# Moving weight loads to a second DMA queue in fp32, with a replanned instruction order, in a pooled-attention and expert-attention kernel

## The chip, the cores and the metric

The kernel runs on one core of one Trainium2 chip. The metric is the device time of one execution in microseconds (us). Executions are sorted into a fast and a slower state, and only fast ones are compared: the ratios leave slow ones out, while the medians quoted are of all runs. Apart from the whole-run time there is the span in the profile, which is about 1.7 us shorter than the time of the same run.

Engine names: TensorE (PE) multiplies matrices, VectorE (DVE) and ScalarE (ACT) evict and compute element by element, GpSimd (POOL) masks and issues loads, SyncE (SP) issues stores. PEld is TensorE's weight load. PEclk is the clock that TensorE was granted, as a share of full speed.

## The reference, cut to what matters

```python
# B=8 batches, H=8 heads, S=576 positions, D=64; fp32 in and out
k_p = k.reshape(B, H, 72, 8, D).mean(axis=3)        # pool k and v by 8
v_p = v.reshape(B, H, 72, 8, D).mean(axis=3)
x = softmax(q @ k_p^T / 8) @ v_p                    # first attention
x = x.transpose(0, 2, 1, 3).reshape(B, S, 512)
logits = x @ w_gate                                 # 4 experts, the best 2 are used
for e in range(4):                                  # causal attention per expert, width 64
    a = softmax(causal((x @ wq[e]) @ (x @ wk[e])^T / 8))
    out += gate[e] * (a @ (x @ wv[e]) @ wo[e])
```

Each batch brings 3.5 MB of fp32 q, k and v. All weights together are 2.1 MB. They are loaded once and first needed after the first attention of batch 0: before that point the kernel needs k, q and v only.

## The kernel before: the parts that matter

The kernel is scheduled by hand. A string of tokens gives the order; each engine executes its own tokens in that order. `L_q3:0` loads chunk 3 of q of batch 0, `W2:0` loads a weight (0 wq, 1 wk, 2 wv, 3 gate, 4 wo), `c` sorts a loaded weight into the layout that TensorE wants, `PK`, `KT`, `Q`, `E`, `D`, `PV`, `O` are the first attention on TensorE (pool k, transpose, transpose q, scores, denominators, pool v, outputs), `V` and `P` the projections of the experts, and small letters the evictions. A `d` at the end puts an eviction on VectorE.

```python
def load(b, nm, c):                       # one chunk of q, k or v
    ...
    nc.gpsimd.dma_start(out=dst, in_=src)   # fp32 in HBM -> bf16 in SBUF: a casting load

def load_weights(i):
    ...
    nc.gpsimd.dma_start(out=dst, in_=src)   # the same queue, also casting

def order_weights(i):                     # bf16 -> bf16 copies, all on VectorE
    ...

SEQ = """
    H:0 M:0 L_k2:0 L_k0:0 I:0 L_k1:0 L_q3:0 L_q2:0 L_q0:0 L_q4:0 L_q5:0 PK:0@0 L_q1:0 kc:0d
    W2:0 KT:0@0 L_v2:0 kt:0d L_v1:0 W3:0 Q3:0@0 Q0:0@1 L_v0:0 r3:0d Q2:0@2 r0:0 Q1:0@3 r2:0d
    ... o11:0 D2:0@3 x0:0 d2:0 o00:0 W1:0 x2:0 o01:0 W0:0 ...   # wk and wq
    ... W4:0 ...                                                # wo, much later
```

`H` is a block of warm-up matmuls that has TensorE at full clock when the first k arrives. So all loads share one queue, in the order in which they are needed: k, q, then wv, v, and the other weights behind.

The softmax here doesn't subtract the row's maximum and nothing guards it: scores larger than these inputs give would overflow.

## Time and profile before

The median of three runs is 180.87 us (180.75 to 182.9). The profiled execution has a span of 178.7 us.

| stage | what happens | length |
|---|---|---|
| 0 to 30 us | the head: loads, first attention of batch 0, clock mostly at half | 30 us |
| 30 to 173 us | TensorE busy 140.7 of 143 us at clock 1.00 | 143 us |
| 173 to 178.7 us | last evictions and stores | 5.5 us |

These are the lines of the profile's page of the kernel before. The second line is busy time (share of the span) and instruction count of each engine; the next two cut the span into 40 slices, in tenths of busy time and of full clock; then the chain of work that ended last, by engine; then the DMA queues with packets, MB written and share of the 16 engines' span.

```profile
span 178.7 us, 5425 instructions
PE 163.2 (91%) x2143; PEld 96.7 (54%) x2143; DVE 123.5 (69%) x408; ACT 140.0 (78%) x251; POOL 106.6 (60%) x183
...
PE   7729689999999999999999999999999999999870
...
PEclk9955556999999999999999999999999999999997
...
PE 71%; DVE 9%; ACT 7%; POOL 4%; issue 3%; DMA 2%; DVEq 0%; POOLq 0%; ACTq 0%
...
q0 software_dynamic: 78928, 15.21, 102.2%
q1 hardware_dynamic: 5248, 9.44, 14.7%
```

TensorE is the bound except in the first six or seven slices; in most of these its clock is halved. Queue q0 carries the casting loads; its MB are those written, and it reads twice as much. Queue q1 here carries the stores alone.

The stretches of the head, kernel before. Columns: stretch, length, busy time (instructions) of PE, PEld, DVE, ACT, POOL, then granted clock, DMA share, GB/s written.

```profile
10.00:15.00 5.00, 2.50 (x27) 2.14 (x28) 1.02 (x4) 0.64 (x1) 5.00 (x7) 0.50 1.91 150
15.00:20.00 5.00, 3.67 (x31) 1.76 (x31) 0.30 (x1) 4.68 (x7) 4.26 (x6) 0.50 1.84 168
20.00:25.00 5.00, 4.10 (x40) 1.24 (x34) 3.44 (x10) 3.04 (x7) 4.66 (x6) 0.50 2.23 162
25.00:30.00 5.00, 4.98 (x47) 3.79 (x47) 2.38 (x7) 0.97 (x4) 3.98 (x6) 0.50 1.84 179
```

The clock is 0.50 all through. Only in the last of these stretches is TensorE itself the limit (4.98 of 5 us busy).

The timeline of TensorE in the head, kernel before. Columns: start, length, engine, line, operation, operands, count, and in brackets the idle time before and what ended it.

```profile
8.71 0.61 PE L204 MATMUL psum<-kraw_71,poolk 96*32 96x512 bf16 x5 [0.99 <-DMA kraw_71<-in_k_dram]
...
13.26 2.02 PE L208 MATMUL psum<-ident,qraw_68 96*128 96x96 bf16 x23 [1.93 <-DMA qraw_68<-in_q_dram]
...
25.36 2.78 PE L204 MATMUL psum<-wvg,xT_97 128*128 128x260 bf16 x12
...
29.12 1.60 PE L208 MATMUL psum<-ident,qraw_69 96*128 96x96 bf16 x24
```

These four are the landmarks: k is there at 8.7 us, the last q at 13.26 us, the first expert projection starts at 25.36 us, and batch 1 follows at 29.12 us.

### The profile page before, as it was taken

The page shows a single profiled execution, that of the slowest core. Times are in us where ns is not written, and L with a number is a line of the kernel's source. Part 1 is how long each engine was busy: PE and PEld are TensorE (multiplying, and loading weights), DVE is VectorE, ACT ScalarE, POOL GpSimd, SP SyncE. Part 2 cuts the span into 40 slices and gives each one's busy share as a digit, 9 for nine tenths or more (in the row PEclk, how much of TensorE's full clock was granted, in tenths as well). Part 3 has the DMA queues.
Part 4 walks back from the last instruction along what each step waited for, and adds up shares of the span by engine and source line. Part 5 has one row for each costly group of instructions (what it writes and reads, how often), then busy time and mean ns, then how long its engine had stood idle before and what let it go on. Part 6 is the DMA issues. An engine that isn't in the chain of part 4 may idle for free.

```text
span 178.7 us, 5425 instructions
## 1 busy us (share of the span) xinstructions
PE 163.2 (91%) x2143; PEld 96.7 (54%) x2143; DVE 123.5 (69%) x408; ACT 140.0 (78%) x251; POOL 106.6 (60%) x183
## 2 busy tenths in 40 slices
PE   7729689999999999999999999999999999999870
PEld 2516147446575565745666566556655555567530
DVE  5022374686789885994898579968998569498860
ACT  2007914899989878989989889988998999997660
POOL 6999797786699788948999538017131202254000
PEclk9955556999999999999999999999999999999997
DMA  3999999999969999999999998950439010200486
GB/s 32 126 140 163 172 165 178 160 158 144 112 70 148 163 236 206 194 173 273 129 135 167 222 189 89 155 207 5 43 117 226 31 59 6 88 0 6 164 306 238
DMA packets 84202, 25.00 MB, mean 140 GB/s; under 512 B 79312, under 2 KB 79568, under 8 KB 84176
## 3 DMA queue, kind: packets, MB, share of 16 engines
q0 software_dynamic: 78928, 15.21, 102.2%
q1 hardware_dynamic: 5248, 9.44, 14.7%
q8 instruction: 16, 0.26, 0.6%
q14 instruction: 10, 0.08, 0.2%
HBM read 30.42 MB, written 9.44 MB: 223 GB/s over the span
## 4 chain that ended last, share of the span: by engine, by line
PE 71%; DVE 9%; ACT 7%; POOL 4%; issue 3%; DMA 2%; DVEq 0%; POOLq 0%; ACTq 0%
PE psum L204 63%; PE psum L208 8%; DMA qraw_68<-in_q_dram 2%; POOL qraw_68 L112 2%; DVE osc_111 L465 2%; ACT eta_91 L270 2%; ACT etb_101 L420 1%; DVE osc_110 L465 1%; POOL kraw_71 L112 1%; ACT lnz_93 L291 1%; DVE xT_97 L313 1%; ACT ofin L201 1%; ACT rza_95 L294 1%; DVE gt_109 L461 1%; DVE gt_108 L461 1%
## 5 line engine op out<-in xcount | busy, mean ns | idle before, releaser
L437 POOL TENSOR_SCALAR_AFFINE_SELECT etb_100<-etb_100 128x256 bf16<-128x256 bf16 x32 | 12.6, 410 | 28.1 <-ACT etb_100 L420 28.0
L420 ACT ACTIVATE etb_101<-psum 128x1024 bf16<-128x1024 f32 x24 | 23.8, 1029 | 4.2 <-PE psum L204 3.5
L420 ACT ACTIVATE etb_100<-psum 128x1024 bf16<-128x1024 f32 x24 | 23.8, 1027 | 1.2 <-PE psum L204 1.1
L437 POOL TENSOR_SCALAR_AFFINE_SELECT etb_101<-etb_101 128x256 bf16<-128x256 bf16 x32 | 12.7, 411 | 19.8 <-ACT etb_101 L420 15.2
L270 ACT ACTIVATE eta_92<-psum 96x1024 bf16<-96x1024 f32 x16 | 15.7, 1021 | 1.0 <-PE psum L204 0.8
L270 ACT ACTIVATE eta_91<-psum 96x1024 bf16<-96x1024 f32 x16 | 15.6, 1019 | 0.3 <-PE psum L204 0.3
L201 DVE CAST qk_103<-psum 128x512 bf16<-128x512 f32 (+1 forms) x16 | 10.3, 653 | 7.9 <-PE psum L204 7.7
L201 ACT COPY ofin<-psum 128x512 f32<-128x512 f32 (+1 forms) x24 | 13.3, 583 | 2.8 <-PE psum L204 2.6
L112 POOL DMA_DIRECT2D qraw_69<-in_q_dram x18 | 13.9, 774 | 1.0 <-DMA vraw_74<-in_v_dram 1.0
L112 POOL DMA_DIRECT2D qraw_68<-in_q_dram x18 | 13.8, 771 | 0.4 <-issue 0.2
L201 DVE COPY ofin<-psum 128x512 f32<-128x512 f32 (+1 forms) x16 | 10.9, 684 | 1.7 <-PE psum L204 1.6
L201 ACT COPY qT_83<-psum 128x576 bf16<-128x576 bf16 x2 | 1.3, 638 | 12.3 <-PE psum L208 12.3
L204 PEld LDWEIGHTS <-etb_101 128*128 128x128 bf16 x240 | 9.0, 97 | 2.9 <-issue 0.9
L204 PE MATMUL psum<-wvg,xT_97 128*128 128x260 bf16 x60 | 10.3, 314 | 0.0
L112 POOL DMA_DIRECT2D qraw_70<-in_q_dram x12 | 9.2, 774 | 1.3 <-DMA wst_q<-in_moe_wq_dram 1.0
L204 PE MATMUL psum<-vaug_105,etb_101 128*128 128x65 bf16 x240 | 9.8, 193 | 0.0
L204 PEld LDWEIGHTS <-etb_100 128*128 128x128 bf16 x240 | 8.5, 97 | 1.9 <-issue 1.0
L204 PE MATMUL psum<-vaug_104,etb_100 128*128 128x65 bf16 x240 | 9.3, 193 | 0.0
L201 DVE CAST qk_102<-psum 128x512 bf16<-128x512 f32 (+1 forms) x10 | 6.3, 636 | 4.0 <-PE psum L204 4.0
L204 PE MATMUL psum<-wvg,xT_98 128*128 128x260 bf16 x60 | 8.5, 275 | 0.3 <-DVE osc_110 L465 0.3
L204 PE MATMUL psum<-qk_103 64*128 64x64 bf16 (+4 forms) x96 | 8.7, 277 | 0.1
L204 PE MATMUL psum<-qk_102 64*128 64x64 bf16 (+4 forms) x96 | 8.4, 276 | 0.0
(247 smaller groups left out, 472.0 us busy)
## 6 DMA issues: line engine op xcount, KB each, us to landing
out_dram<-ofin SPq DMA_DIRECT2D x32, 256.0 KB, 3.2
kraw_71<-in_k_dram POOLq DMA_DIRECT2D x9, 192.0 KB, 4.4
qraw_68<-in_q_dram POOLq DMA_DIRECT2D x18, 96.0 KB, 4.5
vraw_74<-in_v_dram POOLq DMA_DIRECT2D x9, 192.0 KB, 6.4
kraw_72<-in_k_dram POOLq DMA_DIRECT2D x9, 192.0 KB, 6.6
qraw_69<-in_q_dram POOLq DMA_DIRECT2D x18, 96.0 KB, 6.2
vraw_75<-in_v_dram POOLq DMA_DIRECT2D x9, 192.0 KB, 6.7
qraw_70<-in_q_dram POOLq DMA_DIRECT2D x12, 96.0 KB, 7.4
```

The costliest lines, as they stand in the source:

```text
L112: nc.gpsimd.dma_start(out=dst, in_=src)
L201: (nc.vector.tensor_copy if dve else nc.scalar.copy)(out=out, in_=in_)
L204: nc.tensor.matmul(out=out, lhsT=lhsT, rhs=rhs, start=start, stop=stop)
L208: nc.tensor.transpose(out=out, in_=in_, identity=ident[0:n, 0:n])
L270: nc.scalar.activation(out=eta[:, hp, :, 0:MAIN], in_=psum[0:KR, bank : bank + 2, :], func=EXP, scale=ATT_EXP_SCALE,)
L291: nc.scalar.activation(out=part(lnzs[b % 2], g), in_=z, func=LN)
L294: nc.scalar.activation(out=part(rzas[b % 2], g), in_=part(lnzs[b % 2], g), func=EXP, scale=-1.0)
L313: nc.vector.tensor_tensor(out=xT[:, 2 * g + t, 0:MAIN], in0=psum[:, bank, :], in1=rz[:, g, 0:MAIN], op=MULT)
L420: nc.scalar.activation(out=et[:, ep, :, eo : eo + n], in_=psum[:, bank : bank + 2, 0:n], func=EXP, scale=MOE_EXP_SCALE,)
L437: nc.gpsimd.affine_select(out=blk, in_=blk, pattern=[[0, 2], [1, 128]], compare_op=ISGE, fill=0.0, base=0, channel_multiplier=-1,)
L461: nc.vector.tensor_mul(out=gt[:, :, :, 0], in0=rz[:, :, :, 0], in1=at[b, "G"][:, q0:q1, 2 * ep : 2 * ep + 2].rearrange("p c e -> p e c"),)
L465: nc.vector.tensor_tensor(out=oscs[ep][:, q0:q1, :].rearrange("p c (e d) -> p e c d", e=2), in0=o[:, :, :, 0:HD], in1=gt.to_broadcast([128 ...
```

## The change

The intent: take the weights off the GpSimd queue, where they cost issue time and their place in the order; load them in fp32 by SyncE, which is free until the first store, from the beginning; load k, q and v strictly in turn; keep TensorE busy with filler matmuls in the first waits, so that its clock stays up; use ScalarE less in the head; and plan the whole order again, stores included.

```diff
-    wst = {nm: const.tile([128, E, 2, 2, HD], BF16, name=f"wst_{nm}") for nm in ("q", "k", "v")}
+    wst = {nm: const.tile([128, E, 2, 2, HD], FP32, name=f"wst_{nm}") for nm in ("q", "k", "v")}
+    wst_o = const.tile([128, NEP, DM], FP32, name="wst_o")
...
-        nc.gpsimd.dma_start(out=dst, in_=src)          # in load_weights
+        nc.sync.dma_start(out=dst, in_=src)
+    def open_weights(i):                                # token G: lets SyncE start
+        for t in ([wst["q"], wst["k"]], [wst["v"], wst_g, wst_o])[i]:
+            nc.vector.memset(first(t), 0.0)
-    def order_weights(i):                               # bf16 -> bf16 on VectorE
+    def order_weights(i, dve):                          # fp32 -> bf16, on either engine
...
+    def warm_up(n, bank):                               # token H: n filler matmuls
+        for _ in range(n):
+            nc.tensor.matmul(out=psum[:, bank, :], lhsT=warm[:, 0:128], rhs=warm[:], start=True, stop=True)
...
-        H:0 M:0 L_k2:0 L_k0:0 I:0 L_k1:0 L_q3:0 L_q2:0 L_q0:0 L_q4:0 L_q5:0 PK:0@0 L_q1:0 kc:0d
-        W2:0 KT:0@0 L_v2:0 kt:0d L_v1:0 W3:0 Q3:0@0 Q0:0@1 L_v0:0 r3:0d ...
+        I:0 M:0 L_k0:0 L_k1:0 G0:0 W0:0 L_k2:0 G1:0 W1:0 J:0 W2:0 W3:0 K:0 L_q0:0 c1:0 W4:0
+        L_q1:0 L_q2:0 L_q3:0 L_q4:0 L_q5:0 H20:0@7 PK:0@0 kc:0 L_v0:0 H4:0@7 KT:0@0 L_v1:0
+        L_v2:0 L_k0:1 c0:0 H7:0@7 Q3:0@1 kt:0d L_k1:1 r3:0d c2:0 Q2:0@0 r2:0d Q0:0@2 L_k2:1
+        c3:0d Q1:0@3 r0:0d E3:0@4 e3:0 E2:0@0 L_q0:1 r1:0d H4:0@7 E4:0@4 e2:0 E1:0@2 H1:0@7 ...
```

Cut: the whole remaining order is new too; the softmax logarithm is kept in place of its result (one buffer less); the constants need three affine selects instead of six; one eviction of three instructions became three tokens.

## The prediction

> **What bounds the kernel now.** The span is 178.7 us. TensorE is 91% busy and the chain of waits puts 71% of the span on it. By stretches: from 30 us to its last matmul at 173.2 us TensorE is busy 140.9 of 143 us at granted clock 1.00, so this part is TensorE-bound, with about 2 us of waits, 1.1 of them at 160-170 us. The rest is the head (0-30 us) and the tail (5.5 us from the last matmul to the end). The head is a chain, not TensorE-bound: k lands at 8.7 us, the last q at 13.26, ScalarE exponentials from 15.9, first projection at 25.4 us. The stretches show the granted clock at 0.50 from about 9.5 to 30 us: TensorE waited (12-13 us: no busy time) and then worked at half speed. Of the roughly 15 us of busy time that isn't warm-up before 30 us, most would take half.
>
> **What the change removes.** (a) Five weight issues of 0.7-0.9 us on GpSimd, and four affine selects of 0.2-0.3 us each; three stay, now behind the third k load, so k is issued about 1.6 us earlier. (b) The half clock. From 25.4 to 30.3 us the trace has TensorE saturated at 0.50; at 1.00 that saves about 2.5 us. Earlier half-clock work is mostly hidden by ScalarE. (c) Two or more of batch 0's four qT copies (0.64 us each) leave ScalarE before the first exponential: about 1.3 us. (d) Over the whole kernel some 7 us of evictions move from ScalarE (140 busy) to VectorE (123.5), mostly output copies (24 to 17 on ScalarE).
>
> **What it adds.** Weight reordering now reads fp32: three copies of about 0.6 us on ScalarE, in the wait for q, and about 3.5 us on VectorE. About 21 more filler matmuls of 0.22 us sit in waits. The main cost is contention: 2.1 MB of fp32 weights start at about 3-4 us, beside k and q. The Trainium skill, "DMA: Bandwidth & Descriptors", section "Issuing engines are not separate DMA queues", says a second queue only saves issue time. The trace has the casting loads at 140-180 GB/s written from 8 us on (twice that read), so weights are an estimated 6.5 us of transfer time, shared with q. Estimate: q lands near 15-16.5 us instead of 13.3; v near 20, as before.
>
> **On the critical path.** Later q (+2 to +3) roughly cancels the ScalarE relief and earlier k (-2). The first projection starts within 1.5 us of 25.4. What remains: about 2.5 us from the clock, 0.5-1 from smaller mid-kernel waits, 0.5-1 from a less crowded tail (13 stores among the final tokens now, about 11 then, the last one issued at 175.0 although its tile was ready at 173.8). Sum about 4-5 us.
>
> **Prediction: 176.3 us, 80% range 172.0 to 179.5. Chances: faster by over 2% 0.62, within 2% 0.33, slower 0.05.**
>
> **What would show it.** Windows: granted clock 1.00 from about 8 us on, TensorE busy after 30 us still some 141 us in sum. DMA issues: weights land on the SyncE queue by 14-17 us, q's time to landing rises from 4.5 us to above 6. Timeline: first projection at 24-27 us. Chain: ScalarE exponentials in the head, TensorE afterwards.
>
> **What would make it wrong.** The fillers don't hold the clock: "TensorE: Matmul & The Clock Gate", section "What's actually happening", has it halve after an idle window of about 3.4 us, and the trace halved it after a sparser stretch; a 3-4 us wait for q would do so again, and the gain shrinks to 1-2 us. Or weights barely delay q; then the first projection comes at 23 us and the time is 173. Or the new order has new waits around 50-60 us, where VectorE is 96% busy.

## More of the kernel before

The DMA view of the kernel before, cut to 5 to 20 us: the queue, then the q loads of batch 0 with the median time from issue to landing at the end.

```profile
q0 software_dynamic: 11406, 2.18, 176.0%
...
qraw_68<-in_q_dram POOLq DMA_DIRECT2D x6, 96.0 KB, 4.1
```

## The result, and the profile after

After: median 182.94 us (182.67 to 183.38, four runs). Before, in the same rounds: 180.81 us (179.8 to 182.9, four runs). The ratio is 1.0139, with a 95% interval of 1.0091 to 1.0188. Of the kernel before, the run of 182.9 us is 1.7% above the fastest, which counts as slow, and 1.0139 is the ratio of the means without it (with it, it would be 1.0105). A ratio here is the mean time of one kernel's fast runs over the mean of the other's fast runs of the same rounds, so it is not quite the ratio of the medians that are quoted. The kernel became 1.4% slower, which is within 2% but on the wrong side, and the time lies above the predicted range.

The page of the kernel after, the same lines:

```profile
span 181.2 us, 5407 instructions
PE 162.1 (89%) x2100; PEld 93.9 (52%) x2121; DVE 127.4 (70%) x414; ACT 135.4 (75%) x244; POOL 102.2 (56%) x175
...
PE   7655399999999999999999999999999999999970
...
PEclk9978558999999999999999999999999999999996
...
PE 71%; DMA 13%; DVE 6%; POOL 4%; issue 2%; ACT 1%; POOLq 0%; DVEq 0%; ACTq 0%
...
q0 software_dynamic: 75264, 14.16, 94.6%
q1 hardware_dynamic: 8912, 11.55, 19.6%
```

In the chain that ended last, DMA went from 2% to 13% of the span and ScalarE from 7% to 1%. ScalarE lost 4.6 us of work and VectorE gained 3.9, as intended. The weights are now on q1 (11.55 MB less 9.44 MB of stores is 2.11 MB).

The stretches of the head, kernel after:

```profile
10.00:15.00 5.00, 4.05 (x17) 1.45 (x17) 0.36 (x1) 1.62 (x3) 1.58 (x3) 0.66 1.82 192
15.00:20.00 5.00, 1.06 (x8) 0.44 (x5) 0.00 (x0) 0.62 (x1) 1.54 (x2) 0.79 1.56 240
20.00:25.00 5.00, 3.53 (x26) 2.16 (x28) 2.92 (x7) 1.06 (x2) 3.96 (x5) 0.50 1.84 179
25.00:30.00 5.00, 5.00 (x34) 1.46 (x36) 0.69 (x1) 3.69 (x5) 3.94 (x6) 0.68 2.05 139
```

From 15 to 20 us TensorE is busy for 1.06 of 5 us, VectorE not at all and ScalarE for 0.62: everyone waits for data. The fillers raised the clock in parts, but it is back at 0.50 from 20 to 25 us.

The timeline of TensorE in the head, kernel after:

```profile
10.44 0.59 PE L193 MATMUL psum<-kraw_71,poolk 96*32 96x512 bf16 x4 [2.90 <-DMA kraw_71<-in_k_dram]
...
17.38 0.22 PE L197 MATMUL psum<-ident,qraw_68 96*128 96x96 bf16 x1 [1.59 <-DMA qraw_68<-in_q_dram]
19.95 0.26 PE L197 MATMUL psum<-ident,qraw_68 96*128 96x96 bf16 x1 [2.35 <-DMA qraw_68<-in_q_dram]
...
21.61 1.70 PE L197 MATMUL psum<-ident,qraw_68 96*128 96x96 bf16 x19 [0.36 <-DMA qraw_68<-in_q_dram]
...
32.47 0.28 PE L193 MATMUL psum<-xT_95,wqp_119 128*128 128x64 bf16 x4 [0.20 <-DVE xT_95 L296]
```

The last q is there at 21.6 us instead of 13.26, and the first projection starts at 32.5 us instead of 25.4. The last k came later too (10.4 for 8.7 us), although the last k load was issued earlier.

The DMA view of the kernel after, 5 to 20 us:

```profile
q0 software_dynamic: 6772, 1.13, 96.9%
q1 hardware_dynamic: 3663, 2.11, 59.3%
...
qraw_68<-in_q_dram POOLq DMA_DIRECT2D x6, 96.0 KB, 12.0
```

This is the reading that matters most. Before, the core read 2 × 2.18 = 4.36 MB in this stretch (the casting loads write half of what they read). After, it read 2 × 1.13 = 2.26 MB of loads and 2.11 MB of weights, together 4.37 MB. From 8 to 20 us alone, past a lull in the loads of the kernel before at 6 us, it is 3.64 against 3.54 MB. The second queue added no bandwidth for reading: it gave almost half of it to weights that nobody needed before 25 us. A load of a q chunk took 12.0 us to land instead of 4.1.

The lateness of 7 us at the first projection became only 2.5 us of span. From 30 us on, TensorE had 140.9 us of work before and 142.2 after (some matmul records can be missing from a trace), so by 30 us the new order was behind by little in TensorE work, though it was behind by much in its chain. Which part of the new order does this was not separated.

### The profile page after: what moved, and what is told of

It is laid out like the page before. It is cut to its first block, busy times and chain, and to the rows that moved or that the text cites. A ratio compares the mean times of both kernels' runs of the same rounds, so it can differ in the third digit from the quotient of the medians.

```text
span 181.2 us, 5407 instructions
## 1 busy us (share of the span) xinstructions
PE 162.1 (89%) x2100; PEld 93.9 (52%) x2121; DVE 127.4 (70%) x414; ACT 135.4 (75%) x244; POOL 102.2 (56%) x175
## 3 DMA queue, kind: packets, MB, share of 16 engines
q1 hardware_dynamic: 8912, 11.55, 19.6%
HBM read 30.42 MB, written 9.44 MB: 220 GB/s over the span
## 4 chain that ended last, share of the span: by engine, by line
PE 71%; DMA 13%; DVE 6%; POOL 4%; issue 2%; ACT 1%; POOLq 0%; DVEq 0%; ACTq 0%
PE psum L193 62%; PE psum L197 8%; DMA qraw_68<-in_q_dram 7%; DMA qraw_69<-in_q_dram 3%; DMA qraw_70<-in_q_dram 3%; POOL qraw_68 L112 2%; PE psum L187 2%; POOL kraw_71 L112 1%; DVE xT_95 L303 1%; DVE ofin L190 1%; DVE vaug_103 L190 1%; DVE osc_109 L458 0%; ACT rza_93 L284 0%; DVE W L349 0%; DVE qk_101 L190 0%
## 5 line engine op out<-in xcount | busy, mean ns | idle before, releaser
L427 POOL TENSOR_SCALAR_AFFINE_SELECT etb_98<-etb_98 128x256 bf16<-128x256 bf16 x32 | 12.5, 409 | 26.1 <-ACT etb_98 L410 25.7
L427 POOL TENSOR_SCALAR_AFFINE_SELECT etb_99<-etb_99 128x256 bf16<-128x256 bf16 x32 | 12.5, 410 | 19.4 <-ACT etb_99 L410 18.6
L190 DVE COPY ofin<-psum 128x512 f32<-128x512 f32 (+1 forms) x23 | 15.1, 682 | 2.2 <-PE psum L193 2.2
L187 PE MATMUL psum<-warm 128*128 128x512 bf16 x40 | 13.4, 485 | 1.6 <-DVE poolk L151 1.3
L197 PE MATMUL psum<-ident,qraw_68 96*128 96x96 bf16 x72 | 5.8, 227 | 5.1 <-DMA qraw_68<-in_q_dram 5.1
L112 POOL DMA_DIRECT2D kraw_72<-in_k_dram x9 | 6.9, 769 | 4.3 <-DMA qraw_68<-in_q_dram 4.3
L193 PE MATMUL psum<-qk_101 64*128 64x64 bf16 (+4 forms) x96 | 9.2, 277 | 0.0
L187 PEld LDWEIGHTS <-warm 128*128 128x128 bf16 x41 | 4.4, 117 | 9.2 <-issue 6.0
L193 PE MATMUL psum<-vaug_103,etb_99 128*128 128x65 bf16 x240 | 8.6, 193 | 0.1
L193 PE MATMUL psum<-wvg,xT_96 128*128 128x260 bf16 x60 | 8.7, 274 | 0.0
L193 PEld LDWEIGHTS <-etb_99 128*128 128x128 bf16 x240 | 8.0, 97 | 1.2 <-issue 1.2
L112 POOL DMA_DIRECT2D vraw_74<-in_v_dram x9 | 6.9, 771 | 2.9 <-DMA qraw_68<-in_q_dram 2.1
```

Source lines behind the costliest of these rows:

```text
L187: nc.tensor.matmul(out=psum[:, bank, :], lhsT=warm[:, 0:128], rhs=warm[:], start=True, stop=True)
L190: (nc.vector.tensor_copy if dve else nc.scalar.copy)(out=out, in_=in_)
L193: nc.tensor.matmul(out=out, lhsT=lhsT, rhs=rhs, start=start, stop=stop)
L197: nc.tensor.transpose(out=out, in_=in_, identity=ident[0:n, 0:n])
L427: nc.gpsimd.affine_select(out=blk, in_=blk, pattern=[[0, 2], [1, 128]], compare_op=ISGE, fill=0.0, base=0, channel_multiplier=-1,)
```

## The experiments

**Theory 1 (contention):** the weights in fp32 on the second queue take the bandwidth that k and q need, and this alone turns a gain into a loss. **Rival A (copies):** the weight copies, now on ScalarE and waiting for slow weights (10.03 us at the first one, and the eviction of pooled k stands behind it), hold the head. **Rival B (plan):** the new order or the fillers are worse by themselves. **Rival C (format):** it is fp32 instead of casting, not the queue.

### 1. The new plan with the weights back on the loads' queue (a_wcast)

```diff
-        nc.sync.dma_start(out=dst, in_=src)     # staging FP32
+        nc.gpsimd.dma_start(out=dst, in_=src)   # staging BF16
- ... G0:0 W0:0 L_k2:0 G1:0 W1:0 J:0 W2:0 W3:0 K:0 L_q0:0 c1:0 W4:0 ...
+ ... L_q5:0 W2:0 H20:0@7 ... L_v1:0 W3:0 L_v2:0 W0:0 W1:0 L_k0:1 ...
+ ... o20:0 c0:0 c1:0d c2:0 c3:0d PK:1@0 ... L_v2:1 W4:0 ...
```

> The changed kernel, but the weights go back to bf16 casting loads on the GpSimd queue in the places they had before (wv after q, gate between the v loads, wq and wk after v, wo later); their reorder copies come later to fit. Theory 1 (the early fp32 weights take half of the transfers while q streams in): the last q lands at 13-14 us instead of 21.6, first projection at 23-25 us instead of 32.5, and since the rest of the changed kernel needs 143 us to its last matmul, the time is 174-177 us. Theory 2 (the replanned order itself is worse, the weights don't matter): first projection still after 28 us, time 181-184 us.

Measured: 177.76 us against 179.58 before in the same rounds, ratio 0.9882 (0.9822 to 0.9942). The timeline of TensorE in this kernel:

```profile
12.49 0.98 PE L197 MATMUL psum<-ident,qraw 96*128 96x96 bf16 x19 [0.46 <-DMA qraw<-in_q_dram]
26.24 0.61 PE L193 MATMUL psum<-xT,wqp 128*128 128x64 bf16 x8
```

The last q is there at 12.5 us and the first projection starts at 26.2. Both the projection (expected at 23 to 25 us) and the time (174 to 177) miss theory 1's figures a little, but are far from those of the rival. With the weights back in their place in one queue, the plan of the kernel after is faster than the kernel before. That speaks for theory 1 and against rival B.

### 2. Only the second queue, in the old plan (b_wsp)

```diff
- ... L_k0:0 I:0 L_k1:0 ...
+ ... L_k0:0 I:0 G:0 W0:0 W1:0 W2:0 W3:0 W4:0 L_k1:0 ...   # fp32, by SyncE
- W2:0 / W3:0 / W1:0 / W0:0 / W4:0 at their old places
+ c3:0                                  # one more copy on VectorE, for wo
```

(The logarithm is kept in place, as in the change, to make room for the fp32 staging.)

> The kernel before, with nothing changed but the weights: fp32 on the SyncE queue, released at about 3.4 us. Theory 1: q lands after 19 us instead of 13.3, first projection 5-8 us later, time 185-188 us. Theory 2: within 1 us of 180.8.

Measured: 188.29 us against 179.58, ratio 1.0458 (1.0396 to 1.0519); the median is just above the expected 185 to 188. TensorE's two landmarks, its waits (total, times, longest), and the queues from 5 to 20 us in this kernel:

```profile
20.45 2.02 PE L215 MATMUL psum<-ident,qraw 96*128 96x96 bf16 x23 [1.86 <-DMA qraw<-in_q_dram]
32.20 2.78 PE L211 MATMUL psum<-wvg,xT 128*128 128x260 bf16 x12
...
PE psum L215 <- DMA qraw<-in_q_dram: 5.2, 2, 3.3
PE psum L211 <- DMA kraw<-in_k_dram: 5.0, 1, 5.0
...
q0 software_dynamic: 7102, 1.19, 102.1%
q1 hardware_dynamic: 3664, 2.11, 55.6%
```

The last q comes at 20.45 us and the first projection starts at 32.20, so the head is moved as in the kernel after, with the old order and none of its new copies on ScalarE. Queue q0 wrote 1.19 MB from 5 to 20 us and q1 2.11 MB, nearly the division of the kernel after. The early loads on the second queue alone are enough for the damage. In the old plan they cost 4.6%. In the new plan they cost about 2.6% (1.0139 against the 0.9882 of a_wcast, from different rounds): the plan itself gains the 1.2% of a_wcast, and only the rest of the difference is delay that the new order hides.

### 3. Only the copies later (a_clate)

```diff
- ... L_q0:0 c1:0 W4:0 ... L_k0:1 c0:0 H7:0@7 ... r3:0d c2:0 Q2:0@0 ... L_k2:1 c3:0d Q1:0@3 ...
+ ... o20:0 c0:0 c1:0d c2:0 c3:0d PK:1@0 ...
```

> The changed kernel with its early fp32 weights, only the reorder copies moved behind the first batch's exponentials, so that ScalarE no longer waits for wq before it evicts the pooled k. Theory 1: kp is evicted at about 11 us instead of 12.6, but q still lands at 21-22 us and the time stays within 1 us of 182.9. Theory 2 (ScalarE waiting for weights is the cause): 2-4 us faster.

Measured: 183.38 us, ratio 1.0216 (1.0169 to 1.0263) against the kernel before. TensorE's waits for q add up to 7.9 us. ScalarE no longer waits for weights in front of pooled k, and nothing is won. Rival A falls.

### 4. The second queue, but started later (a_wlate, a_wlate2)

```diff
- ... G0:0 W0:0 L_k2:0 G1:0 W1:0 J:0 W2:0 W3:0 K:0 L_q0:0 c1:0 W4:0 ...
+ ... r0:0d G1:0 G0:0 W2:0 W3:0 W0:0 W1:0 W4:0 E3:0@4 ...    # SyncE starts once q is transposed
+ ... o20:0 c0:0 c1:0d c2:0 c3:0d PK:1@0 ...                # a_wlate2: c4:0d moved here too
```

> The changed kernel, fp32 weights still on the SyncE queue, but released only when q of the first batch has been transposed and copied; reorder copies later. Theory 1: q lands at 13-14 us; the weights now share with v and the second batch, so PV is 1-3 us later than in the run with casting weights; time 175-179 us. Rival (it is the SyncE queue or the fp32 copies that cost, not when the weights are sent): no gain over the changed kernel, 181-184 us.

> The late release on the SyncE queue again, without the flaw of the first try, where the copy of wv stood ahead of the eviction of the pooled v on VectorE and held it 6 us: now all reorder copies come after the outputs of the first attention. Theory 1: the pooled v is evicted at about 17 us, but weights that share with the second batch's loads land late (wk near 29 us, as in the first try), so the first projection is at 28-31 us and the time 179-182 us. If the second queue were harmless once q is in, first projection at 23-25 us and 175-177 us.

Measured: a_wlate 183.01 us, ratio 1.0204 (1.0153 to 1.0255). Theory 1 had expected 175 to 179, so this was a miss, and the rival's figure, 181 to 184, was met. Partly it was a fault of the edit: the copy of wv stood ahead of the eviction of pooled v on VectorE, and wv landed late, so TensorE waited 6.2 us for pooled v. The second edit took that away and still has 183.05 us, ratio 1.0205 (1.0112 to 1.0298), a little above its expected 179 to 182. So a late start does not make the second queue harmless. The waits of TensorE in a_wlate2, and its queues from 14 to 30 us:

```profile
PE psum L193 <- ACT wqp L190: 5.4, 1, 5.4
PE psum L193 <- ACT wkp L190: 2.5, 1, 2.5
...
q0 software_dynamic: 7460, 1.34, 102.5%
q1 hardware_dynamic: 3509, 1.82, 54.9%
```

In a_wcast, in the same stretch, all of it through one queue:

```profile
q0 software_dynamic: 13385, 2.71, 195.2%
```

Here q is in time (12.5 us), and now the weights are late: the copies of wq and wk release the first projections. From 14 to 30 us this kernel read 2 × 1.34 MB of loads and 1.82 MB of weights, 4.50 MB together; a_wcast read 2 × 2.71 = 5.42 MB in the same stretch through one queue. The two queues moved not even as much as one. So theory 1 needs a sharper form. The point is not that weights must keep away from q. All loads up to the first projection share one bandwidth, and a second queue beside a full first one shares it with loads of the next batch that are not yet due, whichever of the two is wanted first. In one queue the order of the tokens decides, and a_wcast has an order that fits the deadlines. (This reading is argued from the two kernels; no run changed the sharing alone.)

### 5. fp32 or the queue (a_wpool32)

As a_wcast, with the staging in fp32 and the copies casting: plain loads of 512 KB, in the GpSimd queue.

```diff
-        nc.sync.dma_start(out=dst, in_=src)     # staging FP32, order as in a_wcast
+        nc.gpsimd.dma_start(out=dst, in_=src)
```

> As the run with casting weights (177.8 us), in the same places of the GpSimd queue, but the weights stay fp32 and are cast by the reorder copies. If what counts is where the weights stand in the order of transfers and not the cast: q lands at 12-13 us, time 177-178.5 us. If the fp32 format itself costs (twice the bytes written, slower copies): 179-183 us.

Measured: 179.18 us, ratio 0.9979 (0.9898 to 1.006). The last q is there at 12.36 us and the first projection starts at 26.39, as in a_wcast. So fp32 does not make the loss (rival C falls as its cause); the second queue does, with the place in the order of transfers that it gives the weights. Whether fp32 costs about 1% against casting stays open: the time lies in the range expected for a format that costs (179 to 183), but the intervals of the two ratios overlap, and they ran on different chips.

### 6. The fillers and the clock (a_nofill, b_fill)

```diff
- H4:0@7 H7:0@7 H4:0@7 H1:0@7 H4:0@3 H1:0@3       # a_nofill: after, without these 21 fillers
+ F5 before PK, F4 before KT, F9 before Q3, F4 before D1, F2 before PV, F2 before O01
                                                  # b_fill: before, with 26 such fillers
```

> The changed kernel without its 21 filler matmuls (only the first 20 stay). If the fillers hold the clock: half speed from about 11 us until 28-30 us, time 0.5-2 us longer than 182.9. If, as the changed kernel's windows suggest, the long wait for q drops the clock anyway and ScalarE bounds this stage: within 0.7 us of 182.9.

> The kernel before with 26 filler matmuls of 512 columns in its waits for k, kp, q, the exponentials and vp, nothing else. If the half clock from 25 to 30 us costs what was predicted (2.5 us): granted clock 1.00 through 10-30 us and 177.5-179 us. If the clock falls all the same, or the saved time is lost to ScalarE and VectorE waits: within 0.7 us of the kernel before.

Measured: a_nofill 183.64 us, ratio 1.0187 (1.0109 to 1.0265). Its clock is 0.50 from 15 to 30 us, so the fillers do act on the clock. By medians they are worth 183.64 − 182.94 = 0.7 us here (from different rounds; one of the four runs is slow, and without it the difference is 0.5), which the intervals don't tell from nothing. b_fill has 179.7 us, ratio 0.9973 (0.9907 to 1.0039): no gain shown, where I had predicted 2.5 us (1.4%) from the clock; the interval leaves room for 0.9%. The stretch of b_fill that answers to the saturated one of before:

```profile
25.00:30.00 5.00, 4.20 (x66) 3.10 (x65) 3.97 (x11) 1.58 (x6) 4.01 (x6) 1.00 1.83 180
```

The clock is 1.00 there, and TensorE no longer fills the stretch: its first projection started at 26.57 us, 1.2 later than before, with the last q at 14.54 us in this run, 1.3 later; why q came later isn't shown. What the clock gave, the head took back; batch 1's q transposes start at 28.93 us, 0.2 earlier than before.

### 7. A repaired version, and what limits it (a_best, a_best0, a_best_skipv, b_skipv)

a_best0 is a_wcast with wq and wk moved behind the whole k of batch 1. a_best adds 12 more fillers where its clock fell.

```diff
- ... L_v2:0 W0:0 W1:0 L_k0:1 ... L_k2:1 Q1:0@3 ...
+ ... L_v2:0 L_k0:1 ... L_k2:1 W0:0 W1:0 Q1:0@3 ...          # a_best0, against a_wcast
+ ... H4:0@7 PK:1@0 kc:1 H8:0@7 P_t0:0@4 ...                 # a_best only
```

> The same without the 12 extra fillers. If the clock bounds the stage of 24-30 us: 1-2 us slower than the run with them. If it doesn't, as the kernel before with fillers suggests: within 0.7 us of it.

> The changed kernel with casting weights on the GpSimd queue, as in the 177.8 us run, but wq and wk go behind the second batch's k instead of ahead of it, and 12 more filler matmuls stand in the wait before the first projection. In the 177.8 us run TensorE waited 2.8 us for that k from 21.5 to 25.3 us and its clock was at 0.50 from about 24 to 30 us. Expected: pooling of the second k at 20-22 us, first projection limited by wk at 24-26 us, 175.5-177.5 us. If the place of wq and wk among the loads doesn't matter (their bytes only move): 177.8 again.

Measured: a_best0 177.48 us, ratio 0.9869 (0.9829 to 0.9909); a_best 177.91 us, ratio 0.9864 (0.9824 to 0.9905). Both give the right result, and both beat the kernel before (180.07 us in these rounds) by 1.3%, and the kernel after. a_best missed its expected 175.5 to 177.5 and came out where its rival had it, at 177.8 again. The two are equal, although a_best has the clock at 1.00 from 25 to 30 us where a_best0 has 0.50, and starts batch 1's exponentials 2.5 us earlier (30.04 for 32.52 us). The head start is gone in the stretch from 60 to 80 us. First a_best, then a_best0:

```profile
60.00:80.00 20.00, 17.27 (x269) 11.36 (x270) 14.89 (x49) 16.03 (x32) 17.66 (x29) 1.00 1.74 192
```

```profile
60.00:80.00 20.00, 18.84 (x282) 12.31 (x284) 16.12 (x51) 17.97 (x38) 18.81 (x30) 1.00 1.86 203
```

And the waits of TensorE for q from 35 to 100 us, first a_best, then a_best0:

```profile
PE psum L197 <- DMA qraw<-in_q_dram: 2.6, 5, 1.2
```

```profile
PE psum L197 <- DMA qraw<-in_q_dram: 1.1, 3, 0.6
```

The kernel that arrives earlier waits longer for the loads: 1.5 us of the 2.5 are accounted for by these waits, all of them between 60 and 80 us. To test whether loads are the limit there, I took away the v loads of batches 2 and 3; those batches pool batch 0's v instead, so the result is wrong (relative error 0.695). The same removal in the kernel before is the control.

```diff
-        pool_pe(b, bank, vraws[b % NRAW], poolv)
+        pool_pe(b, bank, vraws[0 if b in (2, 3) else b % NRAW], poolv)
- L_v0:2 L_v1:2 L_v2:2 L_v0:3 L_v1:3 L_v2:3
```

> Wrong results on purpose: the 177.9 us kernel (casting weights, wq and wk behind the second k, extra fillers) without the six v loads of batches 2 and 3; their pooling reads batch 0's v instead, so TensorE, ScalarE and VectorE do the same work. If the start it gained (2.2 us ahead at 35 us of its twin without extra fillers) is given back because loads now arrive too late: the waits for q at 60-80 us (2.6 us between 35 and 100 us) fall under 0.7 us, and it is 2-3 us faster, 175-176 us. If those waits only stand in for another limit: within 1 us of 177.9.

> Control, wrong results on purpose: the kernel before without the same six loads. Its TensorE waits for no load after 35 us, so on the theory it gains nothing: within 1 us of the kernel before. If fewer loads help whatever the order (less SBUF or GpSimd traffic): 2-3 us faster too.

Measured: a_best_skipv 173.97 us, ratio 0.9678 (0.9633 to 0.9724); b_skipv 179.79 us, ratio 0.9998 (0.9958 to 1.0037). The same stretch of a_best_skipv:

```profile
60.00:80.00 20.00, 20.00 (x300) 13.03 (x298) 16.39 (x55) 19.45 (x40) 17.51 (x28) 1.00 1.68 190
```

TensorE is now busy for all of it. TensorE's waits for q between 35 and 100 us are gone. The gain is more than the 2 to 3 us expected: 177.91 − 173.97 = 3.9 us by medians, about 3.4 by the ratios (different rounds). In the kernel before, the six loads cost nothing that the runs show, which fits that it gets there later. So there is a second limit, the loads of batches 2 and 3, that takes back part of what a faster head gains; whether it is their transfer or GpSimd's time to issue them was not separated.

## Why the prediction was wrong, point by point

1. **"q lands near 15-16.5 us instead of 13.3; v near 20, as before" failed, and it decided the case.** The mechanism was named; its size was off. The last q landed at 21.6 us, 8.3 late instead of 2 to 3. I had worked out 6.5 us of transfer time for the weights and then charged q with less than half of it. But the weights were issued from 3.45 us on, beside k and q, and all of them had landed by 20.4 us, while q was still coming in. Two smaller errors add to it. The 6.5 us took about 323 GB/s of reading (2.1 MB in 6.5 us); the trace has 4.37 MB in 15 us, which is 291 GB/s, so the weights take 7.2 us. And q0 wrote 1.41 MB from 5 to 21.6 us, more than all of k and q of batch 0 together (1.18 MB): part of v or of the next k was moved ahead of the last q chunk. The test of the size is b_wsp: the weights' queue alone, in the old order, brought the last q at 20.45 us, 7.2 us late, and +4.6%. The test of the other side is a_wcast: the change without it, −1.2% against before. So of the 6.6 us between the predicted 176.3 and the measured 182.94, about 5 are the queue's (182.94 − 177.76, from different rounds); the rest belongs to points 3 and 5.

   The Trainium skill, "DMA: Bandwidth & Descriptors", section "Issuing engines are not separate DMA queues", says that transfers of all issuing engines run on the same 16 DMA engines and interleave. The trace fits it: 4.36 MB before and 4.37 MB after in the same 15 us. I quoted this and did not take it to its end. If the sum is fixed, then every byte of weights that moves before the last q delays it. The same page, section "Queues, rings and completion order", says that each DMA engine goes round the queue rows that have work, one packet at a time. Over 15 us the two queues read about as much, 2.26 MB against 2.11, but the trace shows no even turns: from 8 to 10 us q0 moved 224 packets and q1 1,015, from 12 to 14 us 1,887 and 212. Whether both had work queued all the time is not in the trace, so how the share is decided stays open.

2. **"Granted clock 1.00 from about 8 us on" failed.** It was 0.66, 0.79, 0.50 and 0.68 in the four stretches from 10 to 30 us. This was the risk that the prediction named, a wait of 3 to 4 us, only that the first one was for k and not for q: TensorE had no work from 7.54 to 10.44 us, and the clock fell at about 11.1 us; it came back at 14.5 us and fell again at 17.9, after the wait of 1.59 us for q and at the beginning of that of 2.35. The Trainium skill, "TensorE: Matmul & The Clock Gate", section "What's actually happening", gives an idle window of about 3.4 us for the drop. The three changes of the clock here are 3.4 us apart, but the stretches before the two drops were not empty: TensorE was busy for 0.66 us in the first and for 1.51 in the second.

3. **"About 2.5 us from the clock" failed too, apart from point 2.** The sum took a half-clock stretch that TensorE filled and halved it. b_fill restored the clock there and gained nothing that the runs can show (0.9973, interval 0.9907 to 1.0039), though its later q makes this a weak test. a_best against a_best0 won 2.5 us at 30 us, the predicted size, and lost it again, 1.5 us of it by waits for loads between 60 and 80 us. The skipv pair shows that the loads of batches 2 and 3 are a limit of the faster kernel and not of the kernel before. A gain in one stage was counted as a gain at the end.

4. **"Weights land on the SyncE queue by 14-17 us" failed in part.** wq landed at about 12.1 us and wk at 15.1, but wv at 18.3 and wo at 20.4 (issue plus time to landing). That the loads of k and q held them up too is likely but not shown: no run has the weights alone.

5. **"0.5-1 from smaller mid-kernel waits, 0.5-1 from a less crowded tail": not there.** The tail from the end of the last matmul to the end is 5.6 us, before 5.5. In the middle there are new waits for q of batches 1 and 2, of 0.5 and 0.4 us.

6. **"Later q roughly cancels the ScalarE relief and earlier k": failed with point 1.** "Earlier k" turned into its opposite: the last k landed 1.7 us later (10.44 for 8.71 us). The relief was real (ScalarE's part of the chain went from 7% to 1%), but it saves nothing while ScalarE waits: it was idle for 8.10 us before its first exponential at 23.94 us.

7. **Right:** the kernel is bound by TensorE after 30 us (140.7 of 143 us); q's time to landing rose above 6 us, though to 12.0; ScalarE lost and VectorE gained about the predicted kind of work, though less of it; and the new order is better than the old, which a_wcast shows once the weights are out of the way.

**What stays open:** why the second queue costs 4.6% in the old order and only about 2.6% in the new one; what the weights would cost early in the GpSimd queue, or late and one by one on SyncE, since no run has them so and the queue and the place in the order changed together; how the DMA engines divide themselves between the two queues, and why both together read less than one casting queue in a_wlate2; and whether fp32 loads in the GpSimd queue cost 1% against casting ones.

## What to carry to other kernels

Before moving transfers to a second queue, add up the bytes that will move before the first deadline: here a queue that was already full gained no bandwidth from a neighbour, and it lost its order of deadlines. Charge a competing transfer in full to whatever it can delay, until a measurement says less. A gain in the head counts only if no later limit takes it back; find that limit by taking some of its work away, with the old kernel as the control.

## What the Trainium skill lacked or had wrong

- "DMA: Bandwidth & Descriptors": how much a plain SyncE load takes from casting GpSimd loads beside it. Here it was 2.11 MB against 2.26 MB read in 15 us, and a casting load of 96 KB landed after 12.0 us instead of 4.1. Nor what the mixture does to the sum, which differed by pair: 4.50 MB read in 16 us in a_wlate2 and 5.42 MB through the casting queue alone in a_wcast, but 4.37 and 4.36 MB in 15 us in the kernels after and before. The cause isn't shown.
- "DMA: Bandwidth & Descriptors", section "Issuing engines are not separate DMA queues", has the time to start a DMA as usually small beside the DMA itself. In the kernel after, on SyncE, the issue of wv (512 KB, landed after 13.6 us) took 4.47 us, and that of the gate weights (8 KB) right behind it 3.17 us, where wq took 0.43.
- No page that I found says that GpSimd's issue of a load waits for earlier loads to land. In the kernel after, issues of v waited once 2.11 us, and those of the next k three times, 4.3 us in all, for q of batch 0. The trace shows the wait, not its reason, which may also lie in the program's own semaphores.
- "TensorE: Matmul & The Clock Gate", section "What's actually happening", speaks of an idle window of about 3.4 us. In the kernel before, the clock fell at about 9.5 us although no gap between matmuls was longer than 0.99 us: TensorE was busy for 0.29 of the microsecond from 8 us and 0.32 of that from 9 us. In the kernel after it fell at 17.9 us, after 3.42 us in which TensorE was busy for 1.51. So sparse work counted as idle here too, and the page does not say how sparse.
